# First MLP of a fused attention and two-MLP kernel: the split rows of w_in are loaded by GpSimd, the V products are stored by SyncE, and the stores of split and decoded weights are pinned

## The chip, the cores and the metric

The kernel runs on one core of a Trainium2 chip. The metric is the device time of one execution in microseconds. Three runs of the kernel before gave 1508.26, 1509.73 and 1510.35 us, so the median is 1509.73 us.

## The reference, in what matters

An attention between 512 tokens and 32 state rows per head comes first (8 batches, 8 heads, head size 64). Its output, 8 x 544 = 4352 tokens of width 512, goes through two MLPs with 2048 hidden columns each.

```python
# per batch and head, x is [512, 64], state is [32, 64]
xread = softmax(x @ state.T / 8) @ state        # 512 rows
sread = softmax(state @ x.T / 8) @ x            # 32 rows
y = concat(xread, sread)                        # -> [4352, 512]
h = y @ w_in                                    # first MLP
g = where(h >= 1, h, where(h <= -1, 0, (h + 1)**2 / 4))
z = g @ w_out
h2 = z @ w_in2                                  # second MLP
out = (max(h2, 0) + alpha * min(h2, 0)) @ w_out2
```

The weights arrive as 64-bit floats.

## The kernel before, in words

**Precision.** Weights are decoded from 64-bit words to float32 on ScalarE and VectorE. Most products are made in three passes: each operand is split into a high and a low part of type float32r (`hi_` casts on ScalarE, `lo_` subtracts on VectorE), and high x high, high x low and low x high are summed in PSUM (`mm3`).

**V products.** The output rows of the attention are `a @ state`, so the first MLP multiplies by `V = state @ w_in` in place of `w_in`: for each batch, V has one row per head and state row (256 rows) and 2048 columns. Batch 0 has its own path. Group 0 (batches 1 to 4) is computed by `vg_dir` from weights in SBUF, in token tile 0. Group 1 (batches 5, 6, 7 and a fourth row block) is computed later: the split weights are stored in DRAM as `wd[blk]` of shape `[2, 512, 512]` (high, low), and for each block of 512 columns and each head, `vg_load` (line 489) loads the 64 rows of the head, high and low, as one tile `ws` of 128 x 512. `vg_mm` multiplies it by the state's high and low parts (two matmuls, lines 510 and 511), and `vg_out` copies the PSUM bank out on ScalarE (`vgo`, line 494) and stores it in the DRAM tensor `vd[g][blk][h]` (line 495). `vr_load` (line 518) reads a batch's rows back, from `vd[g][blk][4q:4q+4, 32i:32i+32, :]`, and `vr_hi` and `vr_lo` split them for the matmuls `hA` of that batch.

**Order.** Work goes in steps `i` = 16 t + f: token tile t (0 to 7, one batch of 512 tokens each; tile 8 holds the state rows) and block f of 128 hidden columns. A step does `h_mm` of step i + 2 (6 matmuls), the activation, and `out_mm` of step i (12 matmuls into four banks; with float32 operands, 4 of them, in tile 0). At the end of a tile ScalarE copies the four banks out (`oA`, line 627). Everything else hangs on a step by `at(step, fn, ...)` in the dictionary `side`:

- `vg_plan(1, 32, 1.0)` spreads the 32 products of group 1 over the steps 32 to 63, which are tiles 2 and 3. The load hangs at `o - 3`, the product at `o + 1`.
- For batch b, `vr_load` hangs two steps ahead of `vr_hi`; eight loads a batch, during the tile before.
- The weights of the second MLP are loaded (`d_load`, line 375), decoded and summed from step 36 on. `w2o_store` (line 689) stores decoded rows in `wod`, `w_store` (line 686) stores the split products in `w1c` and `w2c`. There are 16 and 112 of these stores, each hung three or four steps after its split or its decoding.
- `prep_bd` makes, on GpSimd, the block-diagonal state of a batch (`bdf`, `bdl`), two steps ahead of its tile. In the second MLP, GpSimd subtracts half of the low parts of the input (`xl`).

**Queues.** `ld` is SyncE; it issues nearly all loads and the V stores of group 0. `pool` is GpSimd; it issues the V stores of group 1, the weight stores above, and most of the output. Each engine works in order: an instruction that waits holds those behind it. The order on each engine is made by the framework's scheduler, which plays the program through with its own estimates and takes, by program order as priority, what is ready in that play. An instruction that has few inputs can thereby move ahead of others on its engine. `tc.keep_in_program_order(ins)` adds an edge that holds `ins` behind the instruction traced just before it on its engine; the edge is one of order and adds no wait.

Of the kernel before, what the change touches and what calls it, by code (L numbers as in the profile page):

```python
# [9 lines left out]
F32 = mybir.dt.float32  # L10
# [21 lines left out]
NB, NH, S, NS, D = 8, 8, 512, 32, 64  # L32
# [8 lines left out]
def kernel_body(ctx: ExitStack, tc: tile.TileContext, x, state, w1i, w1o, w2i, w2o, alpha, out):  # L41
# [9 lines left out]
    def U(name, dt=F32):  # L51
        return up.tile([128, 512], dt, tag="u", name=name)
# [10 lines left out]
    act, dve, pool, pe, ld = nc.scalar, nc.vector, nc.gpsimd, nc.tensor, nc.sync  # L63
# [30 lines left out]
    vd = [[dp.tile([NH, 128, 512], F32, name=f"vd{g}_{k}") for k in range(4)] for g in range(2)]  # L94
    xd = dp.tile([NO, 128, TOK], F32, name="xd")
    w1c = dp.tile([8, 7, 128, 512], F32, name="w1c")
    w2c = dp.tile([7, 8, 128, 512], F32, name="w2c")
    wod = dp.tile([NF, 128, 512], F32, name="wod")
    wd = [dp.tile([2, DM, 512], F32, name=f"wd{k}") for k in range(4)]
# [271 lines left out]
    G = {}  # L371
# [114 lines left out]

    def vg_load(g, blk, h):
        t = U(f"ws{g}{blk}{h}", F32R)
        ld.dma_start(out=t.bitcast(F32), in_=wd[blk][:, h * D:(h + 1) * D, :])
        G["w", g, blk, h] = t  # L490

    def vg_out(g, blk, h, ps):
        o = U(f"vgo{g}{blk}{h}")
        act.copy(o, ps)
        (pool if g else ld).dma_start(out=vd[g][blk][h], in_=o)

    def vg_dir(blk, c):
        for h in (2 * c, 2 * c + 1):
            sh, sl = ST[0, h // 4]
            k = slice((h % 4) * 128, (h % 4) * 128 + 128)  # L500
            ps = PS(f"vgp0{blk}{h}")
            mm3(ps, [(sh[:, k], sl[:, k], *W["wi", blk, c])])
            vg_out(0, blk, h, ps)

    def vg_mm(g, blk, h):
        ws = G.pop(("w", g, blk, h))
        sh, sl = ST[g, h // 4]
        c = (h % 4) * 128
        ps = PS(f"vgp{g}{blk}{h}")
        pe.matmul(ps, sh[:, c:c + 128], ws, start=True, stop=False)  # L510
        pe.matmul(ps, sl[:, c:c + 128], ws, start=False, stop=True)
        vg_out(g, blk, h, ps)
# [33 lines left out]
    def gi(t, f):  # L546
        return t * NF + f
# [134 lines left out]
    def w_store(key, *products):  # L682
        for p in products:
            t = WS.pop((key, p)).bitcast(F32)
            j = key[1]
            pool.dma_start(out=w1c[j, p] if key[0] == "i" else w2c[p, j], in_=t)

    def w2o_store(f):
        pool.dma_start(out=wod[f], in_=G.pop(("dec", ("w2o", f))))


    NSUP = len(HALF)
# [183 lines left out]
    def second():  # L876
# [4 lines left out]
        for j in range(5, 8):  # L881
            n = 6 + 10 * (j - 5)
            later[n - 4].append((w2_get, j))
            later[n].append((w2_sums, j))
            for k, p in enumerate(ORDER):
                later[n + 1 + k].append((w_split, ("o", j), p))
                later[n + 4 + k].append((w_store, ("o", j), p))
# [74 lines left out]
    for b in range(1, NB):  # L962
        t0 = gi(b - 1, 0)
        at(t0 - 2, prep_bd, b)
        for q in range(2):
            o = t0 + 4 * q
# [4 lines left out]
        for blk in range(4):  # L971
            for q in range(2):
                o = t0 + 10 + 4 * blk + q
# [5 lines left out]
    def vg_plan(g, start, per):  # L979
        n = 0  # L980
        for blk in range(4):
            for h in range(NH):
                o = start + int(n * per)
                at(o - 3, vg_load, g, blk, h)
                at(o + 1, vg_mm, g, blk, h)
                n += 1
        at(start - 2, ld_stg, g)
        at(start, st_build, g, 0)
        at(start, st_build, g, 1)
# [9 lines left out]
    for blk in (1, 2, 3):  # L999
        for c in range(4):  # L1000
            o = 4 * blk - 7 + c
# [21 lines left out]
    for n, key in enumerate(w2):  # L1023
        o = gi(2, 4) + int(2.75 * n)
        at(o - 3, d_load, key, src_w2p(*key[1:]) if key[0] == "w2i" else src_w2o(key[1]))
        decode(key, o)
        if key[0] == "w2o":
            at(o + 4, w2o_store, key[1])
        elif key[2]:
            at(o + 2, w1_sums, key[1])  # L1030
            for k in range(4):
                at(o + 3 + 2 * k, w_split, ("i", key[1]), *ORDER[2 * k:2 * k + 2])
                at(o + 6 + 2 * k, w_store, ("i", key[1]), *ORDER[2 * k:2 * k + 2])
# [9 lines left out]
    for j in range(5):  # L1043
        o = gi(7, 2 + 5 * j)
        at(o - 4, w2_get, j)
        at(o, w2_sums, j)
        for k, p in enumerate(ORDER):
            at(o + 1 + k, w_split, ("o", j), p)
            at(min(o + 4 + k, gi(8, 15)), w_store, ("o", j), p)
# [85 lines left out]
```

## Time and profile before

| | |
|---|---|
| median of three runs | 1509.73 us |
| the profiled execution | 1506.12 us |
| its span, first to last instruction | 1504.4 us |
| TensorE busy | 1391.4 us, 92% |
| VectorE busy | 1108.2 us, 74% |
| ScalarE busy | 830.8 us, 55% |
| GpSimd busy | 225.4 us, 15% |
| granted TensorE clock, mean | 0.97 |

Busy time of an engine leaves out its waits and the issue of DMAs by SyncE and ScalarE. The profile cuts the span into 40 slices of 37.6 us and gives a digit for the busy share in each. The DMA share is a mean over 16 DMA engines. Tile 0 ends at 160.3 us, tile 1 at 232.9, tile 2 at 363.6, tile 3 at 501.3, and the first MLP at about 832 us.

### The profile page before, as it was taken

Reading aid. Unit: us, or ns where it says so; the run is one execution under the profiler, and the core shown is the slowest. Engines: PE = TensorE matmul, PEld = TensorE weight load, DVE = VectorE, ACT = ScalarE, POOL = GpSimd, SP = SyncE. Lnnn points to the kernel's source line nnn. Section 1 sums busy time; section 2 is a strip of 40 time slices with the busy share of each in tenths; the row PEclk is TensorE's granted clock in tenths of the full one; section 3 lists DMA queues with packets and bytes.
Section 4 is the critical chain, followed back from the end, with each engine's and each line's share of the span. In section 5 each row is a group of like instructions: output and inputs, shape, how many; then the busy total and the mean of one; then the engine's idle time right before and its main releaser. Section 6 shows DMA issues by size and latency. Waiting matters only on the chain.

```text
span 1504.4 us, 20757 instructions
## 1 busy us (share of the span) xinstructions
PE 1391.4 (92%) x6596; PEld 1175.9 (78%) x6596; DVE 1108.2 (74%) x2089; ACT 830.8 (55%) x1658; POOL 225.4 (15%) x334
## 2 busy tenths in 40 slices
PE   6799998857764999999999999999999999999997
PEld 4466786645653888888789778788888999999997
DVE  7887674725542898987758678868877796797886
ACT  5566775534343767776766556434544463463452
POOL 0000000111110211110125112104210420320300
PEclk9999999979896999999999999999999999999999
DMA  6898323444343553644688896667676887897982
GB/s 219 301 329 263 98 74 113 141 139 168 116 173 118 180 172 130 211 146 160 225 301 280 299 342 183 203 186 252 219 233 211 303 280 238 293 308 223 327 312 56
DMA packets 169373, 320.57 MB, mean 213 GB/s; under 512 B 26416, under 2 KB 41776, under 8 KB 169264
## 3 DMA queue, kind: packets, MB, share of 16 engines
q1 hardware_dynamic: 145440, 260.11, 52.8%
q0 software_dynamic: 16384, 49.30, 8.8%
q10 hardware_dynamic: 7440, 9.83, 1.9%
q8 instruction: 53, 0.87, 0.2%
q14 instruction: 56, 0.46, 0.1%
HBM read 242.10 MB, written 76.55 MB: 212 GB/s over the span
## 4 chain that ended last, share of the span: by engine, by line
PE 63%; DMA 16%; DVE 9%; issue 7%; ACT 3%; POOL 1%; SPq 1%; ACTq 0%; DVEq 0%; POOLq 0%
PE o L823 19%; PE accA L614 13%; PE ha L764 9%; DMA vr<-vd 8%; PE hA L84 8%; PE hb L764 5%; DMA ws<-wd 3%; PE accA L606 3%; PE hc L764 2%; DMA x<-in_x_dram 2%; DVE gs L76 2%; PE vgp L84 1%; DMA w<-w1c 1%; DMA wr_wi<-in_moe_w_in_dram 1%; DVE t L803 1%
## 5 line engine op out<-in xcount | busy, mean ns | idle before, releaser
L823 PE MATMUL o<-gs,w 128*128 128x384 f32 (+1 forms) x1680 | 367.8, 358 | 4.7 <-DVE c L837 3.4
L823 PEld LDWEIGHTS o<-gs,w 128*128 128x128 f32 x1680 | 301.4, 188 | 32.4 <-DVE c L837 4.9
L764 PE MATMUL ha<-xh,w 128*128 128x384 f32 (+1 forms) x640 | 202.2, 358 | 1.4 <-ACT g L783 1.4
L73 ACT CAST gs<-g 128x384 fp32r<-128x384 f32 (+1 forms) x240 | 126.1, 554 | 60.9 <-PE o L823 23.5
L76 DVE TENSOR_TENSOR gs<-g,gs 128x384 fp32r<-128x384 f32 (+1 forms) x240 | 143.1, 626 | 15.5 <-ACT gs L73 15.0
L771 ACT ACTIVATE m<-g 128x384 f32<-128x384 f32 (+1 forms) x120 | 68.2, 568 | 139.3 <-DVE g L787 134.6
L76 DVE TENSOR_TENSOR gl<-g,gh 128x512 fp32r<-128x512 f32 (+1 forms) x128 | 90.0, 703 | 69.2 <-ACT gh L73 67.9
L764 PEld LDWEIGHTS ha<-xh,w 128*128 128x128 f32 x640 | 118.9, 188 | 14.7 <-ACT g L783 4.0
L582 DVE SCALAR_TENSOR_TENSOR g<-y,hA 128x512 f32<-128x512 f32 (+1 forms) x144 | 93.9, 652 | 40.4 <-ACT y L580 39.5
L579 ACT ACTIVATE y<-hA 128x512 f32<-128x512 f32 (+1 forms) x144 | 82.5, 573 | 57.8 <-PE hA L84 57.4
L764 PE MATMUL ha<-xl,w 128*128 128x384 f32 (+1 forms) x320 | 114.2, 357 | 0.0
L873 POOL DMA_DIRECT2D out_dram<-ot x112 | 60.9, 551 | 283.8 <-DVE ot L850 273.0
L764 PE MATMUL hb<-xh,w 128*128 128x384 f32 (+1 forms) x320 | 101.3, 357 | 0.8 <-DVE g L787 0.8
L783 ACT COPY g<-ha 128x384 f32<-128x384 f32 (+1 forms) x120 | 62.6, 521 | 69.7 <-PE ha L764 61.9
L772 DVE SCALAR_TENSOR_TENSOR g<-m,beta_sb,g 128x384 f32<-128x384 f32 (+1 forms) x120 | 80.1, 667 | 23.8 <-ACT m L771 23.1
L73 ACT CAST gh<-g 128x512 fp32r<-128x512 f32 (+1 forms) x128 | 75.7, 591 | 35.1 <-DVE g L582 33.1
L787 DVE TENSOR_TENSOR g<-hb,g 128x384 f32<-128x384 f32 (+1 forms) x80 | 48.5, 606 | 56.2 <-PE hb L764 43.2
L580 ACT ACTIVATE y<-y 128x512 f32<-128x512 f32 (+1 forms) x144 | 87.5, 608 | 4.2
L837 DVE TENSOR_TENSOR c<-o,c 128x384 f32<-128x384 f32 (+1 forms) x100 | 57.8, 604 | 13.4 <-PE o L823 13.2
L764 PEld LDWEIGHTS hb<-xh,w 128*128 128x128 f32 x320 | 59.4, 188 | 7.1 <-DVE g L787 1.7
L606 PE MATMUL accA<-g,wf_w1o 128*128 128x512 f32 x128 | 60.6, 606 | 4.6 <-DVE wf_w1o L399 4.6
L764 PEld LDWEIGHTS ha<-xl,w 128*128 128x128 f32 x320 | 60.1, 188 | 5.7
(975 smaller groups left out, 3260.9 us busy)
## 6 DMA issues: line engine op xcount, KB each, us to landing
w<-w1c SPq DMA_DIRECT2D x280, 256.0 KB
w<-w2c SPq DMA_DIRECT2D x280, 256.0 KB
x<-in_x_dram SPq DMA_DIRECT2D x30, 512.0 KB
vr<-vd SPq DMA_DIRECT2D x56, 256.0 KB
w1c<-wsi POOLq DMA_DIRECT2D x56, 256.0 KB, 5.3
w2c<-wso POOLq DMA_DIRECT2D x56, 256.0 KB, 4.5
wr_wi<-in_moe_w_in_dram SPq DMA_DIRECT2D x16, 512.0 KB
wr_w1o<-in_moe_w_out_dram SPq DMA_DIRECT2D x16, 512.0 KB
```

The source lines that it names most:

```text
L73: act.copy(h, raw)
L76: (eng or dve).tensor_tensor(out=l, in0=raw, in1=h.bitcast(F32), op=ALU.subtract)
L84: pe.matmul(ps, a, b, start=(k == 0), stop=(k == n - 1))
L579: act.activation(out=y[:, :n], in_=ps, func=AF.Relu, bias=0.5, scale=0.5)
L580: act.activation(out=y[:, :n], in_=y[:, :n], func=AF.Square)
L582: dve.scalar_tensor_tensor(out=g[:, :n], in0=y[:, :n], scalar=1.0, in1=ps, op0=ALU.min, op1=ALU.max)
L606: pe.matmul(ACC[k], w[:, k * 128:(k + 1) * 128], g, start=(f == 0), stop=(f == NF - 1))
L614: pe.matmul(ACC[k][:, :n], a, b, start=(f == 0 and j == 0), stop=(f == NF - 1 and j == 2))
L764: pe.matmul(ps, a[:, kk], b, start=(first and m == 0), stop=(m == 5), skip_group_check=True)
L771: act.activation(out=m, in_=h, func=AF.Relu, scale=-1.0)
L772: dve.scalar_tensor_tensor(out=g, in0=m, scalar=beta_sb[:, f:f + 1], in1=h, op0=ALU.mult, op1=ALU.add)
L823: pe.matmul(ps, a, b, start=(p in (0, 4, 1) and jj == 0 and k == 0), stop=(jj == 3 and k == 2), skip_group_check=True)
```

## The change

Three edits. The load of `ws` moves from SyncE to GpSimd, and its target is no longer viewed as float32: it is written as float32r from a float32 source. The V store is on SyncE for both groups. The stores of split and decoded weights stay on GpSimd and are each pinned behind what was traced before them there.

```diff
     def vg_load(g, blk, h):
         t = U(f"ws{g}{blk}{h}", F32R)
-        ld.dma_start(out=t.bitcast(F32), in_=wd[blk][:, h * D:(h + 1) * D, :])
+        pool.dma_start(out=t, in_=wd[blk][:, h * D:(h + 1) * D, :])
         G["w", g, blk, h] = t
 
     def vg_out(g, blk, h, ps):
         o = U(f"vgo{g}{blk}{h}")
         act.copy(o, ps)
-        (pool if g else ld).dma_start(out=vd[g][blk][h], in_=o)
+        ld.dma_start(out=vd[g][blk][h], in_=o)
...
             t = WS.pop((key, p)).bitcast(F32)
             j = key[1]
-            pool.dma_start(out=w1c[j, p] if key[0] == "i" else w2c[p, j], in_=t)
+            tc.keep_in_program_order(pool.dma_start(out=w1c[j, p] if key[0] == "i" else w2c[p, j], in_=t))
 
     def w2o_store(f):
-        pool.dma_start(out=wod[f], in_=G.pop(("dec", ("w2o", f))))
+        tc.keep_in_program_order(pool.dma_start(out=wod[f], in_=G.pop(("dec", ("w2o", f)))))
```

## Rows read from the trace of the kernel before

**Rows 1.** The page: TensorE's busy time, and its slices with the granted clock

```profile
PE 1391.4 (92%) x6596; PEld 1175.9 (78%) x6596; DVE 1108.2 (74%) x2089; ACT 830.8 (55%) x1658; POOL 225.4 (15%) x334
...
PE   6799998857764999999999999999999999999997
...
PEclk9999999979896999999999999999999999999999
```

**Rows 2.** Windows, tiles 2 to 6: length, engines' busy us, clock, DMA share, GB/s

```profile
232.90:363.60 130.70, 95.69 (x385) 75.33 (x383) 62.00 (x113) 59.21 (x116) 15.05 (x26) 0.87 0.40 137
363.60:501.30 137.70, 95.88 (x364) 74.76 (x364) 66.49 (x121) 59.70 (x117) 17.23 (x30) 0.83 0.40 141
501.30:571.70 70.40, 69.54 (x321) 57.75 (x321) 63.17 (x119) 53.24 (x104) 11.67 (x19) 1.00 0.53 185
571.70:643.60 71.90, 71.90 (x333) 59.97 (x332) 64.11 (x118) 52.39 (x100) 7.77 (x12) 1.00 0.49 165
643.60:719.20 75.60, 74.73 (x343) 61.62 (x342) 62.17 (x123) 52.61 (x106) 8.71 (x16) 1.00 0.49 168
```

**Rows 3.** Tile vr, what its readers waited for; then waits of TensorE, 218 to 505

```profile
  DMA vr<-vd: 117.4, 19
...
PE sr L84 <- ACT vgo L494: 20.4, 2, 10.4
```

**Rows 4.** Chain of waits from 215 us on: start, length, what

```profile
222.31 22.64 DMA ws<-wd
245.01 13.14 DMA vr<-vd
...
329.01 21.37 DMA vr<-vd
...
357.47 24.40 DMA ws<-wd
```

**Rows 5.** Timeline of SyncE: start, length of the issues, what

```profile
245.66 12.43 SPq L489 DMA_DIRECT2D ws<-wd  x3
258.18 8.35 SPq L518 DMA_DIRECT2D vr<-vd  x1
```

**Rows 6.** Line 489, the load of ws: issue in ns, shortest, median, longest

```profile
L489 SPq DMA_DIRECT2D ws<-wd x32: 506/2700/6785, 218.7 to 475.7; - x32
```

**Rows 7.** Line 495, the V stores on both queues, with Pool's landing

```profile
L495 SPq DMA_DIRECT2D vd<-vgo x32: 319/326/4492, 54.9 to 133.9; - x32
L495 POOL DMA_DIRECT2D vd<-vgo x32: 542/542/739, 243.0 to 506.0; - x32
...
DMA to landing us min/median/max: 5.1/5.5/6.8
```

**Rows 8.** Windows with SyncE's queue alone in flight, columns as before

```profile
226.00:233.00 7.00, 7.00 (x33) 5.79 (x32) 3.35 (x4) 3.99 (x8) 1.21 (x1) 1.00 0.13 51
...
248.00:250.00 2.00, 2.00 (x11) 1.65 (x10) 0.63 (x3) 1.85 (x4) 0.44 (x1) 1.00 0.26 98
```

**Rows 9.** Chain of waits in tiles 4 and 5, steps without V products

```profile
570.53 2.72 PE accA L614 x12
573.25 1.36 PE hA L84 x6
...
592.30 0.44 PE et L199 x4
```

**Rows 10.** Waits of SyncE, whole run: us in total, times, longest

```profile
SPq L495 <- ACT vgo L494: 35.6, 26, 4.3
```

**Rows 11.** Waits of Pool, 218 to 505: us in total, times, longest

```profile
POOL vd L495 <- ACT vgo L494: 209.2, 28, 19.4
POOL w1c L686 <- DVE wsi L76: 23.5, 13, 7.5
POOL bdl L76 <- ACT bdh L73: 21.7, 3, 15.4
```

**Rows 12.** Groups of instructions: ScalarE's casts in the second MLP

```profile
L73 ACT CAST gs<-g 128x384 fp32r<-128x384 f32 (+1 forms) x240 | 126.1, 554 | 60.9 <-PE o L823 23.5 <-DVE g L800 12.1 <-POOL xl L76 10.0
```

## The prediction

> **What bounds the kernel now.** I read the page's slices first. TensorE is at 9 from slice 14 on, but in slices 7 to 13 it lies between 4 and 8, and the granted clock dips to 6 to 8 among them [rows 1]. So I cut the run at the token tiles of the first MLP, by the instants at which ScalarE copies the sums of a tile out. Tiles 4 and 5 take 70.4 and 71.9 us with TensorE busy in nearly all of it. Tiles 2 and 3 take 130.7 and 137.7 us, with TensorE busy 95.7 and 95.9 us at a clock of 0.87 and 0.83 [rows 2]. These two tiles are the ones into which the 32 V products of group 1 (batches 5 to 8) are woven. They do 32 extra matmuls each, and that can't cost 60 us.
>
> The waits say what is missing. ScalarE stood 117.4 us, 19 times, for `vr` loads, and TensorE's waits point at ScalarE copies that stand in order behind those casts [rows 3]. The chain of waits goes the same way, but its `vr` and `ws` pieces are 13 to 24 us long for 256 KB [rows 4]. Why so long? SyncE's rows: three `ws` issues in a row hold its queue for 12.4 us, and a `vr` behind them is 8.35 us in issue [rows 5]; the median `ws` issue is 2.7 us [rows 6] where a V store from the same queue takes 0.33 us [rows 7]. The queue is full, not waiting for data. And yet the DMA engines are idle: while `ws` alone moves, the share is 0.13 and the rate 51 GB/s [rows 8]. 0.13 of 16 engines is two engines. The tile is loaded from `[2, 64, 512]`, high and low rows, and two is what its slowest dimension allows. So one `ws` is 262144 B / 51 GB/s = 5.1 us on two engines, and 32 of them 164 us. Everything SyncE issues behind one queues on those two engines.
>
> A check by load: the mean share over both tiles is 0.40, so each engine works 0.40 x 268.4 = 107 us. `ws` is 164 x 2/16 = 20.4 of that mean. A `vr` comes from `[4, 32, 512]` and shows 0.26 just after `ws` let go [rows 8]: four engines, 2.6 us each, 16 loads, 41 us on these four and 10 in the mean. The even rest is 107 - 20 - 10 = 77 us. If the pair of `ws` is among the four of `vr`, it has 164 + 41 + 77 = 282 us to do in 268: full. I take that as the bound of both tiles.
>
> **The change part by part.** *`ws` moves to Pool.* SyncE loses 32 issues, and `vr`, `x` and weight loads no longer stand behind them. If Pool's transfers are spread over the engines, the pair loses 164 us and every engine gets 20. Then TensorE is the bound again. One step is 2.72 + 1.36 us [rows 9], all of which, with attention work, is in the 71.15 us mean of tiles 4 and 5. The new length of both tiles: 2 x 71.15 = 142.3; V products 64 matmuls at 2.72/12 = 0.227 us, 14.5; eight transposes of the state at 0.44/4 us, 0.9 [rows 9]; and a residual. Tile 6, with the same loads and Pool's stores, is 75.6 us, 4.45 over that mean; I allow this for each tile, 8.9. Sum 166.6 us against 268.4: 101.8 us gone. Without the residual it is 110.7.
>
> On Pool a load costs an issue of about 0.54 us [rows 7], 32 of them 17 us, in place of 32 V stores at the same price, so Pool's work is level. Pool's transfers in this stretch landed in 5.1 to 6.8 us [rows 7] while SyncE's took 13 to 24, so its queue isn't held by SyncE's backlog. Such a store puts little on each engine; I add the 5.1 us of a pair and estimate 10.6 us for a `ws`. It is traced four steps ahead of its product: 4 x (4.08 + 0.45) = 18.1 us. Margin 7.5 us.
>
> The target of the load is now written as float32r from float32, without the bitcast, which makes a conversion of it. No row has a converting DMA. Lower end: nothing, since the bytes are the same. Upper end: the longest landing that the chain shows for 256 KB, 24.4 us [rows 4], about four times 5.1 us and a store's landing on top. Pool's own landings, 5.1 to 6.8 us [rows 7], are the nearer row, so I take nothing and keep the upper end for a rival.
>
> *V stores move to SyncE.* 32 issues at 0.33 us, 10 us, for 32 that took 2.7 at the median. Each waits for ScalarE's copy of the product, and loads of `vr`, `x` and weights queue behind it. In tile 0 the very same store stood on SyncE: 35.6 us of waiting, 26 times, 4.3 at most [rows 10], with TensorE full. A `vr` is traced two steps, 9 us, ahead of its cast, so 4.3 us leaves half. I take nothing beside the residual; at worst every one of 16 `vr` is 1.4 us (35.6/26) later, 22 us.
>
> *The pins.* 128 stores stay behind what was traced before them on Pool. They add no work. They wait as in program order for VectorE's split, 23.5 us in 13 times here, and `bdl` waits 15.4 us at most [rows 11]; a `ws` behind `bdl` would lose its margin, (15.4 - 7.5) x 3 = 24 us as the upper end. In the second MLP, ScalarE's casts stood 10.0 us for Pool's `xl` [rows 12]: a new order could give these back or add as much, so -10 to +10. TensorE is at 9 there whatever ScalarE does, hence zero.
>
> The profiled execution took 1506.12 us for a span of 1504.4. 1506.1 - 101.8 = 1404.3. The median of the three runs, 1509.73, is 3.6 above the profiled one; on that scale the forecast is **1408 us**. Its own range is 1393 to 1425: 1399 without residual and 6 of the 10 us given back, up to 17 us of the late loads.
>
> The Trainium skill, "DMA: Bandwidth & Descriptors", section "Why a DMA increments its semaphore by 16 and not by 1", says that a load uses the largest count up to 16 that divides both slowest dimensions, always the lowest-numbered engines from SyncE, but consecutive engines from a moving cursor from Pool. The share of 0.13 agrees with the first half; no run here shows the cursor. By it the spread above holds.
>
> **Rivals.** *Same two engines.* Pool's loads land on the pair as SyncE's did. For: the shape is unchanged, and the trace has no Pool load of this shape. Against: nothing but the independence of the queues [rows 7]. The pair keeps its 282 us, whichever queue feeds it, so the stretch stays at 268 give or take 12: 1510 us. The Trainium skill, same page, section "Issuing engines are not separate DMA queues", speaks for this one: all issuers end on the same 16 engines and a second issuer saves issue time alone. By it the time would be about 1510; the trace agrees that issue was blocked, and not that it was all.
>
> *Spread, but late.* The conversion costs four times, or `vr` stays slow. The engines of `vr` then have 77 + 41 + 82 = 200 us in a stretch of 167: 33 us more, 1441. At double cost it is 77 + 41 + 41 = 159 of 167, which fits. For: these four are at 138 of 167 even in my own case. Against: tiles 4 and 5 run full with the same `vr`.
>
> *Slower: Pool's order decides.* Pool is in order, and a `ws` stands behind stores that wait for VectorE, which waits for ScalarE. If the four steps of lead shrink below the 10.6 us of landing, each product waits a landing out: 32 x 10.6 = 339 us, 71 over 268, so 1581. It decides from a lead of 10.6 us down. For: waits of up to 15.4 us on Pool [rows 11]. Against: those were read while the whole stretch stood still for `vr`, and they shrink with it; stores are traced three steps after their split.
>
> **How the numbers follow.** Forecast 0.66; spread but late 0.16; same two engines 0.10; Pool's order 0.08. A difference under 0.2%, 3 us, is about what a measurement of this kernel can tell from none. The second case falls all on faster; the third I split 0.03 faster, 0.03 same, 0.04 slower. Faster 0.66 + 0.16 + 0.03 = 0.85, same 0.03, slower 0.12. The range runs from 1393 over the late case to 1465 (its 1441 and the 24 us of `bdl`), which leaves 0.18 above it and little below.
>
> **What would show it.** Right: tiles 2 and 3 near 83 us each, clock 1.00, no `vr` wait on ScalarE above a few us, SyncE's issues under 1 us, and a DMA share above 0.13 when `ws` alone is in flight. Same engines: both tiles still at 130, Pool's `ws` landing later and later, past 20 us. Late: TensorE's waits name `ws`, with landings of 15 us and more. Order: the same waits, with `ws` issued under 10 us ahead of use and Pool's waits for VectorE before them. Any gain outside tiles 2 and 3 above 10 us would also make my account wrong.

## The result, and the profile after

The changed kernel takes 1402.97 us (median of four runs, 1401.58 to 1406.73), the kernel before 1508.99 us beside it. The ratio is 0.9302, with a 95% interval of 0.9281 to 0.9323. The forecast was 1408 us. The profiled execution took 1401.58 us for a span of 1399.8, against 1506.12 us.

The page of the changed kernel, the lines that answer to [rows 1]:

```profile
PE 1362.9 (97%) x6596; PEld 1160.3 (83%) x6596; DVE 1105.4 (79%) x2089; ACT 831.4 (59%) x1658; POOL 234.1 (17%) x334
...
PE   6799999999999999999999999999999999999997
...
PEclk9999999999999999999999999999999999999999
```

The dip is gone, in TensorE and in its clock. TensorE's busy time fell by 28.5 us without a matmul less, because matmuls that ran at the lower clock in the gaps now run at the full one: in tiles 2 and 3 the granted clock goes from 0.87 and 0.83 to 1.00, and about as many matmuls take 161.2 us in place of 191.6. The windows of tiles 2 to 4, with the columns of [rows 2]:

```profile
232.91:313.83 80.92, 80.92 (x377) 67.55 (x376) 62.16 (x113) 59.38 (x115) 16.20 (x21) 1.00 0.73 206
313.83:395.48 81.65, 80.25 (x367) 65.76 (x366) 64.69 (x121) 59.79 (x118) 20.13 (x28) 1.00 0.84 248
395.48:466.64 71.16, 70.92 (x329) 58.94 (x328) 62.87 (x119) 53.35 (x104) 12.04 (x19) 1.00 0.52 184
```

Tiles 2 and 3 together went from 268.4 us [rows 2] to 162.6, which is 105.8 us. The two profiled executions differ by 104.5 us, so the whole gain lies there. From the end of tile 3 to the end of the run it is 1003.1 us before and 1004.3 after.

The DMA engines now do the same bytes in 60% of the time: shares of 0.73 and 0.84 stand where 0.40 stood. Share times length makes 128 us of work for each engine, against 107 in the prediction's count of the kernel before, so the bytes move sooner but take more engine time. How the `ws` loads run on Pool, in two short windows of the changed kernel (columns as before): one load alone, then four issued between 227.2 and 231.2 us.

```profile
208.50:212.50 4.00, 4.00 (x19) 3.30 (x19) 2.61 (x5) 2.70 (x6) 1.03 (x1) 1.00 0.15 49
232.00:234.00 2.00, 2.00 (x10) 1.69 (x9) 0.96 (x2) 1.94 (x4) 0.00 (x0) 1.00 0.62 147
```

One load still has the pace of two engines, 49 GB/s where [rows 8] has 51. But with four in flight and nothing else moving they run at 147 GB/s and a share of 0.62, ten engines, so they are not all on one pair. This agrees with the moving cursor that the Trainium skill states for loads from Pool ("DMA: Bandwidth & Descriptors", "Why a DMA increments its semaphore by 16 and not by 1").

The issues of `ws` and `vr`, the landings of `ws` (a landing is the time from the issue to the arrival of the data), and the time that readers of `vr` waited for it (views of lines and tiles, as in [rows 3, 6, 7]):

```profile
L489 POOL DMA_DIRECT2D ws<-wd x32: 778/798/988, 205.4 to 373.0; - x32
...
DMA to landing us min/median/max: 8.2/11.3/19.5
```

```profile
L518 SPq DMA_DIRECT2D vr<-vd x56: 509/537/839, 115.2 to 623.9; - x56
```

```profile
  DMA vr<-vd: 5.4, 7
```

The longest `vr` issue fell from 8.35 us in [rows 5] to 0.84, and the waits for `vr` from 117.4 us to 5.4. SyncE waits longer for ScalarE's copies of the products than it did in tile 0 [rows 10], and `vr` is not late by it (218 to 420 us: us in total, times, longest):

```profile
SPq L495 <- ACT vgo L494: 77.8, 27, 4.6
```

### The profile page after: what moved, and what is told of

The parts are those of the page before. It is cut to its first block, busy times and chain, and to the rows that moved or that the text cites. A ratio compares the mean times of both kernels' runs of the same rounds, so it can differ in the third digit from the quotient of the medians.

```text
span 1399.8 us, 20734 instructions
## 1 busy us (share of the span) xinstructions
PE 1362.9 (97%) x6596; PEld 1160.3 (83%) x6596; DVE 1105.4 (79%) x2089; ACT 831.4 (59%) x1658; POOL 234.1 (17%) x334
## 3 DMA queue, kind: packets, MB, share of 16 engines
q0 software_dynamic: 47104, 49.42, 11.1%
## 4 chain that ended last, share of the span: by engine, by line
PE 63%; DVE 8%; DMA 4%; issue 1%; ACT 1%; DVEq 0%; SPq 0%; ACTq 0%
PE o L823 18%; PE accA L614 16%; PE ha L764 10%; PE hA L84 9%; PE hb L764 5%; PE hc L764 2%; DVE gs L76 2%; DMA w<-w1c 2%; DMA w1c<-wsi 1%; DVE g L787 1%; DVE t L803 1%; DMA xst<-xsf 1%; PE sr L84 1%; DVE g L772 1%; PE sc L84 1%
## 5 line engine op out<-in xcount | busy, mean ns | idle before, releaser
L494 ACT COPY vgo<-vgp 128x512 f32<-128x512 f32 x64 | 37.3, 587 | 46.9 <-PE vgp L84 21.6
```

## The experiments

Theory A: the bound of tiles 2 and 3 is the two DMA engines on which every `ws` load sits when SyncE issues it. Rival B: the bound is SyncE's in-order queue, and what helps is to take the loads out of it. View C: the V stores' move is a part of the gain. All runs are compared with the kernel before, run beside them.

**e1: the queue unchanged, the load spread.** Kernel before; the load stays on SyncE, as two loads of 64 rows.

```diff
-        ld.dma_start(out=t.bitcast(F32), in_=wd[blk][:, h * D:(h + 1) * D, :])
+        for k in range(2):
+            ld.dma_start(out=t.bitcast(F32)[k * D:(k + 1) * D, :], in_=wd[blk][k, h * D:(h + 1) * D, :])
```

> Kernel before, but each ws load is issued on SyncE as two loads of 64 rows instead of one of [2, 64, 512]; nothing moves to Pool. Theory A (the bound is two DMA engines that carry every ws load): the two halves spread over all engines, SyncE's queue no longer fills, tiles 2 and 3 take about 81 to 84 us each, total 1400 to 1410 us. Rival B (the bound is SyncE's in-order queue, and what helps is to take the ws loads out of it): the queue now has 64 issues instead of 32, tiles 2 and 3 stay at 131 and 138 us or grow, total 1505 us or more.

Measured: 1405.27 us, ratio 0.9321 (0.9299 to 0.9343). Tiles 2 and 3, and the issue of the halves:

```profile
234.74:319.26 84.52, 83.39 (x385) 68.64 (x383) 61.99 (x113) 59.52 (x115) 14.98 (x26) 1.00 0.67 215
319.26:398.16 78.90, 78.10 (x358) 64.60 (x359) 63.75 (x121) 59.93 (x117) 17.16 (x29) 1.00 0.69 232
```

```profile
L490 SPq DMA_DIRECT2D ws<-wd x64: 444/546/1194, 220.6 to 378.9; - x64
```

Twice the issues in the same queue, and the median issue is 0.55 us where one load took 2.7 [rows 6]. B falls: the queue was only full because two engines emptied it. Nearly the whole gain, 103 us of 106, is had without Pool.

**e4: the queue changed, the load as it was.** Kernel before; `ws` is issued from ScalarE's DMA queue in the same shape.

```diff
-        ld.dma_start(out=t.bitcast(F32), in_=wd[blk][:, h * D:(h + 1) * D, :])
+        act.dma_start(out=t.bitcast(F32), in_=wd[blk][:, h * D:(h + 1) * D, :])
```

> Kernel before, ws loads issued from ScalarE's DMA queue in the same shape; no other edit. A: the same two engines carry them (share near 0.13 when alone), ws loads still take 5.1 us each plus what vr and the rest take on these two, so tiles 2 and 3 stay near 260 to 280 us together and ScalarE is held in issue besides: 1490 to 1530 us. B: SyncE's queue is free, vr lands early, tiles 2 and 3 near 81 to 90 us each: 1400 to 1425 us.

Measured: 1510.97 us, ratio 1.0020 (1.0010 to 1.0029). The tiles keep 133.6 and 131.0 us; the third line is a stretch in which ScalarE's queue alone moves data, again with the share of two engines:

```profile
233.76:367.37 133.61, 102.66 (x390) 78.48 (x388) 61.67 (x113) 59.95 (x115) 14.96 (x26) 0.87 0.40 139
367.37:498.41 131.04, 92.78 (x349) 70.21 (x350) 65.40 (x121) 59.73 (x117) 17.31 (x30) 0.86 0.41 146
...
325.00:327.00 2.00, 1.76 (x8) 1.76 (x9) 1.98 (x4) 0.53 (x2) 0.00 (x0) 0.50 0.13 50
```

And this is where the time stands now, in waits of ScalarE and TensorE in these tiles:

```profile
ACT gh L73 <- issue: 42.7, 8, 11.2
ACT wf_w2i L382 <- issue: 33.9, 5, 15.6
```

```profile
PE accA L614 <- ACT gh L73: 36.0, 16, 4.9
```

The waits for `vr` are down to 9.4 us in all, the wait on which the kernel before stood, and not one microsecond is won. The loads fill ScalarE's queue as they filled SyncE's (their longest issue is 11.7 us) and hold ScalarE itself. The Trainium skill says that all issuers end on the same 16 engines, and that another issuer saves only time of issue ("DMA: Bandwidth & Descriptors", "Issuing engines are not separate DMA queues"). For ScalarE this run agrees; for loads of this shape on Pool the measurement decides against the second half, since e2 below gains 97 us by the move alone. One reservation: ScalarE, unlike SyncE, computes, so part of this run's time is its own hold-up, and how much is not shown; e1 is the clean half of the pair.

**e8: half of the loads spread.** As e1, for column blocks 2 and 3 alone, which are the loads of tile 3.

```diff
-        ld.dma_start(out=t.bitcast(F32), in_=wd[blk][:, h * D:(h + 1) * D, :])
+        for k in range(2) if blk > 1 else ():
+            ld.dma_start(out=t.bitcast(F32)[k * D:(k + 1) * D, :], in_=wd[blk][k, h * D:(h + 1) * D, :])
+        if blk < 2:
+            ld.dma_start(out=t.bitcast(F32), in_=wd[blk][:, h * D:(h + 1) * D, :])
```

> Kernel before on SyncE throughout; only the ws loads of the column blocks 2 and 3 (16 of 32, for tile 3) are split in two halves, those of blocks 0 and 1 stay as one load of [2, 64, 512]. A: tile 2 keeps its 131 us, tile 3 falls to 82 to 92 us, total 1453 to 1465 us. B: both tiles stay slow, 1505 us or more.

Measured: 1456.12 us, ratio 0.9653 (0.9639 to 0.9667).

```profile
234.46:366.59 132.13, 97.03 (x385) 76.17 (x383) 61.97 (x113) 59.20 (x115) 14.96 (x26) 0.86 0.42 144
366.59:452.85 86.26, 82.76 (x358) 67.62 (x359) 65.88 (x121) 59.77 (x117) 16.93 (x29) 0.94 0.66 212
```

Each tile answers to its own loads: the price is local, and half the loads are half the gain.

**e2 and e3: the first and the second edit alone.** e2 is the kernel before with the `ws` load on Pool; e3 the kernel before with the V stores on SyncE.

```diff
# e2
-        ld.dma_start(out=t.bitcast(F32), in_=wd[blk][:, h * D:(h + 1) * D, :])
+        pool.dma_start(out=t, in_=wd[blk][:, h * D:(h + 1) * D, :])
# e3
-        (pool if g else ld).dma_start(out=vd[g][blk][h], in_=o)
+        ld.dma_start(out=vd[g][blk][h], in_=o)
```

> Kernel before with the first edit alone: ws loads on Pool with the conversion, V stores of group 1 stay on Pool, no pins. A: nearly the whole gain, 1400 to 1412 us; Pool's ws loads now stand behind V stores that wait for ScalarE, so a few us may be lost. B: the same, as the loads leave SyncE's queue. A third view, C (the V stores' move is a part of the gain): 1430 us or more.

> Kernel before with the second edit alone: V stores of group 1 on SyncE, ws loads stay on SyncE. A: the pair keeps its load, no gain, 1505 to 1520 us. B: SyncE has 32 more in-order waits in a full queue, slower, 1515 to 1540 us. C: a gain of 20 us or more.

Measured: e2 1411.09 us, ratio 0.9356 (0.9342 to 0.9370); e3 1508.30 us, ratio 1.0003 (0.9993 to 1.0012). The load's move is 97 of the 106 us. The store's move by itself is nothing, so C falls. What is left over, 8 us between e2 and the changed kernel, went to the next runs.

**e5, e9, e10: the pins.** e5 is the changed kernel without them; e9 the changed kernel with the V stores of group 1 back on Pool, pins kept; e10 the kernel before with the pins alone (the lines of e5, the other way).

```diff
# e5
-            tc.keep_in_program_order(pool.dma_start(out=w1c[j, p] if key[0] == "i" else w2c[p, j], in_=t))
+            pool.dma_start(out=w1c[j, p] if key[0] == "i" else w2c[p, j], in_=t)
-        tc.keep_in_program_order(pool.dma_start(out=wod[f], in_=G.pop(("dec", ("w2o", f)))))
+        pool.dma_start(out=wod[f], in_=G.pop(("dec", ("w2o", f))))
# e9
-        ld.dma_start(out=vd[g][blk][h], in_=o)
+        (pool if g else ld).dma_start(out=vd[g][blk][h], in_=o)
```

> Changed kernel without the pins: ws loads on Pool, V stores on SyncE, the weight stores free to move. If the pins matter, the weight stores move ahead and ws loads stand behind their waits for VectorE: 1408 to 1425 us. If they don't (my forecast gave them nothing), 1400 to 1406 us, as the changed kernel.

> Changed kernel with the V stores of group 1 back on Pool: ws loads on Pool, pins on. If the pins are what makes the 6 us between the changed kernel (1403) and the one without pins (1409), this is at 1401 to 1406 us. If the V stores' move to SyncE carries it (on Pool they hold the ws loads behind ScalarE's copies), 1408 to 1415 us.

> Kernel before with the pins alone. There is no load on Pool then that a store could hold up, and tiles 2 and 3 are bound by the two engines: 1505 to 1511 us, no difference. A gain of 5 us or more would mean that the pins work by themselves, through the order of the stores and the buffers that they free.

Measured (e5 and e9 are compared here with the changed kernel's 0.9281 to 0.9323): e5 1409.16 us, ratio 0.9344 (0.9328 to 0.9361); e9 1408.76 us, ratio 0.9331 (0.9318 to 0.9344); e10 1506.99 us, ratio 0.9985 (0.9976 to 0.9994). My expectation of e9 went by one cause alone and was wrong: by the medians neither edit brings the last 6 us by itself, with the load on Pool, and both together do. The intervals part e5 from the changed kernel, barely, and those of e9 still overlap by a little, so the V stores' share is the less certain. Why their move helps beside the pins is not shown: the longest landing of a `wsi` store is 12.6 us in e9 and 12.5 in the changed kernel. In e10 the pins are worth 0.15%, at the edge of what can be told.

Where e5 loses them: tile 3 takes 90.9 us where it took 81.65 (in the profiled execution, at 1413.5 us the longest of the four). From its chain of waits in that stretch, and from ScalarE's waits there:

```profile
315.81 18.72 DMA w1c<-wsi
```

```profile
ACT y L579 <- DMA w1c<-wsi: 10.3, 1, 10.3
```

ScalarE's `y` needs a buffer (tiles of this size share 80), and the buffer is still being read by a weight store that took 18.7 us to land, against 5.4 at the median. Two `ws` loads were issued on Pool just before that store, at 310.5 and 311.3 us, and the second landed only after 22.4 us. Once issued, a store waits for no data; I read the 18.7 us as the store queueing, on some of its engines, behind the 5 us that each load needs on its two. The trace allows a second reading: from 310 to 335 us all the engines of e5 are nearly full, and not only two. That stretch in e5, then in e12 of the next pair:

```profile
310.00:335.00 25.00, 20.70 (x92) 16.81 (x90) 13.96 (x22) 11.99 (x23) 6.07 (x8) 0.98 0.97 250
310.00:335.00 25.00, 25.00 (x112) 20.71 (x111) 18.60 (x34) 18.92 (x35) 6.61 (x13) 1.00 0.75 255
```

**e11 and e12: the loads spread on Pool.** Changed kernel, `ws` as two plain loads of 64 rows on Pool, with pins (e11) and without (e12, whose second edit is that of e5).

```diff
-        pool.dma_start(out=t, in_=wd[blk][:, h * D:(h + 1) * D, :])
+        for k in range(2):
+            pool.dma_start(out=t.bitcast(F32)[k * D:(k + 1) * D, :], in_=wd[blk][k, h * D:(h + 1) * D, :])
```

> Changed kernel, each ws load issued on Pool as two plain loads of 64 rows, so that no load sits on two engines for 5 us. If the weight stores on Pool land late because a ws load is ahead of them on two of their engines (12.5 us in the chain of the changed kernel, 18.7 without pins), landings of ws fall from 11.3 to 6 to 8 us, no store on the chain takes over 8 us, and the time is 1397 to 1402 us. If not, 1402 to 1408 us, for 32 more issues on Pool.

> The kernel of e11 without the pins. If the pins mattered only through stores that queue behind loads on two engines, there is nothing left for them: 1397 to 1403 us, as e11. If they matter through the order of the waits on Pool, 5 us or more above e11, as it was between the changed kernel and e5.

Measured: e11 1403.92 us, ratio 0.9312 (0.9299 to 0.9324); e12 1403.37 us, ratio 0.9306 (0.9293 to 0.9320). The landings of `ws` in e11, then those of the `wsi` stores of e12:

```profile
DMA to landing us min/median/max: 2.5/4.2/7.1
```

```profile
DMA to landing us min/median/max: 2.3/5.2/8.0
```

With no load on two engines, no `wsi` store takes over 8.6 us in either run, and the pins make no difference. So the pins matter only beside such loads. That they matter through the stores' late landings fits, but it is argued: spreading the loads also took the share of that stretch from 0.97 to 0.75 at the same rate, and how a pinned order makes a landing do less harm no run shows. The time of e11 lies 2 us above the range that I gave for a yes and in the one for a no: it is no faster than the changed kernel, although that one has landings of up to 12.5 us. e12 lies 0.4 us above its range. With the landings gone, the chain of e11 in tile 3 shows a `vr` of 13.8 us in their place.

**e6: the conversion.** Changed kernel, the target viewed as float32.

```diff
-        pool.dma_start(out=t, in_=wd[blk][:, h * D:(h + 1) * D, :])
+        pool.dma_start(out=t.bitcast(F32), in_=wd[blk][:, h * D:(h + 1) * D, :])
```

> Changed kernel, ws loads on Pool as a plain copy (the target viewed as float32 again): same order on every engine, no conversion. The conversion costs issue on Pool (0.80 us a load measured, 0.54 for a store): that should fall to about 0.54 to 0.6 us, and the landing from 11.3 to about 10 us. Time: 1400 to 1404 us, no difference that can be told, since nothing waited for ws; if landings decide, 3 us or more below the changed kernel.

Measured: 1402.38 us, ratio 0.9294 (0.9281 to 0.9306): no difference that can be told. The landing falls from 11.3 to 10.7 us, but the issue stays at 0.79 us, against my expectation. So the longer issue isn't the conversion's; in e11, where each load has 64 rows, it is 0.53.

**e7: everything on SyncE.** Kernel before with the halves of e1 and the store of e3.

```diff
-        ld.dma_start(out=t.bitcast(F32), in_=wd[blk][:, h * D:(h + 1) * D, :])
+        for k in range(2):
+            ld.dma_start(out=t.bitcast(F32)[k * D:(k + 1) * D, :], in_=wd[blk][k, h * D:(h + 1) * D, :])
-        (pool if g else ld).dma_start(out=vd[g][blk][h], in_=o)
+        ld.dma_start(out=vd[g][blk][h], in_=o)
```

> Kernel before with ws as two loads of 64 rows on SyncE and the V stores of group 1 on SyncE too; Pool keeps only the weight stores, not pinned. Theory A (two engines were the bound): 1398 to 1408 us, at or a little below the changed kernel. Rival B (SyncE's queue is the bound): it now carries all of it, 96 issues and 32 waits, 1505 us or more.

Measured: 1407.76 us, ratio 0.9333 (0.9320 to 0.9346). SyncE carries all of it at a median issue of 0.47 us per half. B is out once more as the main cause. The time is in the range, but 5 us above the changed kernel, where I had it at or below. e12 differs from e7 in this alone, that its halves are on Pool (0.9293 to 0.9320); so at most about 4 us are left for SyncE's queue, and the two intervals touch. Of all versions none is clearly below the changed kernel; the ratios of e1, e6, e11 and e12 lie within its interval.

## Why the prediction was right

**The bound.** Read rightly, and the step that carried it was the share of 0.13 [rows 8]: a wait of 117 us for `vr` and a queue that was full both pointed at SyncE, and only the share told that the queue was the effect and two engines the cause. e1 and e4 are the two sides of it: the same queue with the load spread wins 103 us, another queue with the same two engines wins nothing. That the pair was full is worked out, 282 us of work in 268, and no view shows engines one by one; shown is that to spread these loads alone takes the time away, tile by tile (e8).

**The sum.** 166.6 us were forecast for tiles 2 and 3, 162.6 measured. The residual was the term that was too large. The step price, V products and transposes make 157.7 us; 4.9 were left over where I had allowed 8.9. The sum had no term for what loads and stores do to each other on Pool, and without the pins it would have needed one of about 6 us (e5).

**The load on Pool.** Issue was taken at 0.54 us and is 0.80; landing at 10.6 and is 11.3, 19.5 at most. Both were under the 18.1 us of lead but for that one, and TensorE's waits from 218 to 420 us name no `ws`. That 10.6 came so near is partly luck: it was made for one load in flight, and the first load, with little beside it, landed in 8.2 us; the median of 11.3 has several loads side by side.

**The V stores.** Taken as nothing; in the kernel before that is so (e3, 1.0003). Beside the load on Pool and the pins their move is about 6 us by the medians (e9), with intervals that overlap a little. Their waits on SyncE are 77.8 us where group 0 had the 35.6 of [rows 10], none over 4.6, and `vr` was not late. SyncE's issues in these tiles stayed under 1 us for `vr`, as the sign had it, but not for every V store (2.3 us at most).

**The pins.** Taken as nothing, with 24 us as the upper end by way of a late `ws`. They are worth about 6 us in this kernel (1409.2 against 1403.0), by another way than mine: in e5 a late store that holds a buffer, not a late load. My account had Pool's transfers land in 5.1 to 6.8 us whatever else was in flight. The stores of `wsi` take up to 12.5 us in this kernel and 18.7 in e5; with the loads spread, 8.6 at most (e11).

**The rivals.** *Same two engines*: not so on Pool (0.62 with four in flight), quite so on ScalarE's queue (0.13 in e4). *Spread, but late*: no wait of this kind. *Pool's order*: no `ws` came too late by it; what Pool's order costs without the pins is 6 us, by way of the stores, in place of 71.

## What to carry to other kernels

When a queue is full and the DMA share is low, multiply: share times 16 is the number of engines that work. Here loads with a slowest dimension of 2 alone showed 0.13, two engines; with one of 4 in flight too, it was 0.26, four. Look at the shape of the load before the queue that it stands in; splitting it into two DMAs of 64 rows cost one line and brought 103 of the 106 us. And look at what is ordered behind such a transfer on its new queue too: here stores issued after it landed as late as 18.7 us, and held buffers for so long.

## What was not expected of the hardware

- The conversion from float32 to float32r splits packets: Pool's queue has 47104 of them with it and 30720 without (e6), 512 more per load of 256 KB, and the landing is only 0.6 us longer.
- A Pool issue of 128 rows loaded takes 0.80 us, of 64 rows 0.53, of 128 rows stored 0.54.
- On ScalarE a DMA issue into a full queue holds the engine itself: up to 11.7 us in e4.
- A store on Pool that lands in 5.4 us at the median took 18.7 in e5, after two loads that use two engines each, with all 16 engines at a share of 0.97.
